# A two-layer MLP in seven-product form on one Trainium2 core: the second layer starts its products in another order

## The chip, the cores and the metric

The kernel runs on one core of a Trainium2 chip, in one launch. Its time is device microseconds (us) from start to end, the median of three runs. The core has TensorE (PE in the profile; PEld is its loading of weights), VectorE (DVE), ScalarE (ACT), GpSimd (POOL) and SyncE (SP), whose queue SPq issues the DMAs here. Each engine works through its own instructions in the order in which they were written down, and waits on semaphores for the others.

## The reference

An attention layer, a first MLP with a layer norm, and then the second MLP, of which this document tells:

```python
def _moe2_ref(x, w_in, w_out):          # x: 4608 x 512, w_in: 512 x 2048, w_out: 2048 x 512
    h = x @ w_in
    g = h * (1.0 / (1.0 + np.exp(-1.702 * h)))
    return (g @ w_out).astype(np.float32)
```

## The kernel before

The first part (attention and first MLP, until about 536 us) leaves x in HBM. The second part takes the 4608 tokens in 12 blocks of 384. Both matrix products of a block are done by a seven-product scheme: operands are cut into quarters (`Q11, Q21, Q22, Q12`), seven sums of quarters (called p1 to p7 here, by the number in the code) are multiplied instead of eight pairs. Each of the seven operands is held as two fp16 halves (a rounded value, "high", and what rounding left, "low"), and three matmuls (`PASSES`) make one product of them. A weight's seven forms are prepared once (`w2i`, `w2o`); the token side is made anew in each block.

**A block.** Its w_in product is cut into four units u0 to u3 (`Up`), each 256 hidden columns wide, and its w_out product is one unit dn (`Down`), which contracts over all four. A product of an Up unit is 12 matmuls (2 output halves x 2 slices x 3 passes), one of dn is 48 (8 slices k0 to k7; k0 and k1 need u0, k2 and k3 u1, and so on). So a block has 4 x 7 x 12 + 7 x 48 = 672 matmuls of 192 columns, all written at L1290, and one small fp32 matmul at L378.

**Accumulation.** PSUM bank a of a unit collects p1, then p6, p7 and p4 on top of it; bank b holds p2, bank d p5 and then p3. Between two products on bank a, ACT copies the sum so far into a quarter of the SBUF tile `c` (`snap`, L1300), and DVE adds bank b or d to a quarter (`add`, L1303). The next product on that bank has to wait for that copy. Q11 = p1+p2, Q12 = p1+p6+p5+p3, Q22 = p1+p6+p7+p5, Q21 = p1+p6+p7+p4.

**After an Up unit.** When `c` is whole, ACT computes the gated activation of all four quarters (`gate`, L1325) into slots 0 to 3 of a work tile `w_g`; slots 0 to 2 (`FIRST`) are the operands of p1, p2 and p3 as they stand, "direct quarters". Four subtractions on POOL (`combos`, L333 to L336; on DVE for u3) make slots 3 to 6 (`REST`), the operands of p7, p5, p6 and p4. ACT casts to fp16 high halves (`high`, L1334), DVE makes the low halves (`low`, L1337), each for FIRST and REST apart. dn multiplies them.

**The next block's tokens** (`nxt`) go through the same between the units: four DMAs load y (L355), DVE takes its largest value (L329) and makes a diagonal (L372), a matmul spreads it (L378, "spread"), DVE derives scales (L383 to L388, "rescale"), four subtractions on POOL make `w_y`, and ACT (L411) and DVE (L414) make the halves `ys`. The output of dn leaves by four DMAs on SP (`store`, L1364).

**Order.** The second part is in manual order: each engine's instructions stand as the code calls them in the loop below. Tiles rotate in pools: `psa` 3 banks, `psb` 2, `psd` 3, 3 buffers of `c`, 2 of `work`, 1 of each `g`; a tile's first writer waits for the last reader of the tile that held its buffer. In a block, PE's order is: u0 p1, p2; dn of the block before p7; u0 p6, p5; dn p4; u0 p7; dn p3; then for u1, u2, u3: p1, p2, (last unit's p4), p6, (last unit's p3), p5, p7; then dn p1 on k0 to k2 (18 matmuls), u3 p4, u3 p3, the rest of dn p1 and p2 on k0 to k3, p5 on k0 to k3, p1 and p2 on k4 to k7, p5 on k4 to k7, p6.

Of the kernel before, what the change touches and what calls it, by code (L numbers as in the profile page):

```python
# [8 lines left out]
F32 = mybir.dt.float32  # L9
# [9 lines left out]
P = 128  # L19
# [72 lines left out]
NS = 7  # L92
# [188 lines left out]
def moe_kernel(ctx: ExitStack, tc: tile.TileContext, qT, kT, vT, w_in, w_out, g_ln, w2_in, w2_out, eye, outT):  # L281
# [952 lines left out]
    with ExitStack() as ph:  # L1234
# [14 lines left out]
        class Unit:  # L1249


            def open(self, which, ks):
                k0 = ks[0] == 0
                for p in which:
                    if k0:
                        if p == 1:
                            self.a = psa.tile([P, 2, TH], F32, name="bank_a")
                            self.c = sb.tile([P, 4, 2, TH], F32, name="c")
                        elif p == 2:
                            self.b = psb.tile([P, 2, TH], F32, name="bank_b")  # L1260
                        else:
                            self.d = psd.tile([P, 2, TH], F32, name="bank_d")
                    last = ks[-1] == self.kc - 1
                    self.product(p, {1: "a", 2: "b", 5: "d"}[p], ks, k0, last)
                    if last and p == 1:
                        self.snap(Q11, self.a)
                    elif last and p == 2:
                        self.add(Q11, self.b)

            def more(self, p, begun=False):  # L1270
                self.product(p, "d" if p == 3 else "a", range(self.kc), False, True, True)
                if p == 6:
                    self.snap(Q12, self.a)
                elif p == 7:
                    if begun:
                        self.add(Q22, self.a)
                    else:
                        self.snap(Q22, self.a)
                        self.add(Q22, self.d)
                elif p == 4:  # L1280
                    self.snap(Q21, self.a)
                else:
                    self.add(Q12, self.d)

# [195 lines left out]
```

## Time and profile before

| | us |
|---|---|
| three timed runs | 1253.4, 1254.3, 1257.36 |
| median | 1254.3 |
| span of the profiled execution, first to last instruction | 1251.5 |
| first part, until the last matmul of its kind | about 536 |
| blocks 1 to 10, from u0's first product to the next block's | 58.8 each, three of them 59.0 to 60.8 |
| last block, to the last matmul | 69.9 |

For the profiled execution only its span is known, no time of its own around it; the span stands 2.8 us under the median of the runs. A row of a timeline gives start, duration, engine, line, operation, what it writes and reads, how many were merged, and in brackets how long the engine had been idle and who released it. A merged row of matmuls ends with the modelled end of the last; the rate is read from the starts of two rows that follow each other. The profiled clock is that of TensorE, 1.00 being 2.4 GHz.

### The profile page before, as it was taken

The page shows a single profiled execution, that of the slowest core. Times are in us where ns is not written, and L with a number is a line of the kernel's source. Part 1 is how long each engine was busy: PE and PEld are TensorE (multiplying, and loading weights), DVE is VectorE, ACT ScalarE, POOL GpSimd, SP SyncE. Part 2 cuts the span into 40 slices and gives each one's busy share as a digit, 9 for nine tenths or more (in the row PEclk, how much of TensorE's full clock was granted, in tenths as well). Part 3 has the DMA queues.
Part 4 walks back from the last instruction along what each step waited for, and adds up shares of the span by engine and source line. Part 5 has one row for each costly group of instructions (what it writes and reads, how often), then busy time and mean ns, then how long its engine had stood idle before and what let it go on. Part 6 is the DMA issues. An engine that isn't in the chain of part 4 may idle for free.

```text
span 1251.5 us, 27586 instructions
## 1 busy us (share of the span) xinstructions
PE 1143.5 (91%) x11678; PEld 989.6 (79%) x11678; DVE 730.9 (58%) x1153; ACT 766.5 (61%) x1073; POOL 664.7 (53%) x696
## 2 busy tenths in 40 slices
PE   2778998899999999889999999999999999999998
PEld 2335665576666666789999999999999898999998
DVE  7898877587677843136455454637272737364543
ACT  6998998788789855345445353627263536454552
POOL 5887998687879953424333352525262515243331
PEclk9989999899999999999999999999999999999999
DMA  9979999999989698470101010100011010101000
GB/s 324 302 205 240 269 270 256 248 231 248 256 206 234 164 230 236 109 270 8 46 14 39 14 40 20 33 27 27 27 33 46 7 46 8 46 7 46 14 14 26
DMA packets 246524, 152.85 MB, mean 122 GB/s; under 512 B 163584, under 2 KB 226176, under 8 KB 244096
## 3 DMA queue, kind: packets, MB, share of 16 engines
q1 hardware_dynamic: 246400, 151.09, 45.5%
q8 instruction: 91, 1.49, 0.5%
q14 instruction: 33, 0.27, 0.1%
HBM read 77.66 MB, written 33.55 MB: 89 GB/s over the span
## 4 chain that ended last, share of the span: by engine, by line
PE 30%; POOL 12%; DVE 8%; ACT 8%; issue 5%; DMA 0%; ACTq 0%; POOLq 0%
PE bank_a L1290 18%; PE bank_d L1290 8%; ACT w_g L1325 6%; DVE g L1337 5%; POOL w_g L336 3%; PE bank_b L1290 3%; POOL w_g L335 3%; POOL w_g L333 2%; POOL w_g L334 2%; PE psy L512 2%; ACT g L1334 1%; DVE c L1303 1%; POOL zs L475 1%; DVE w_g L333 0%; ACT c L1300 0%
## 5 line engine op out<-in xcount | busy, mean ns | idle before, releaser
L1290 PEld LDWEIGHTS <-w2i 128*128 128x128 f16 x4032 | 337.4, 98 | 34.3 <-issue 33.7
L1290 PEld LDWEIGHTS <-w2o 128*128 128x128 f16 x4032 | 335.0, 98 | 7.4 <-issue 6.8
L333 POOL TENSOR_TENSOR w_g<-w_g 128x384 f32<-128x384 f32 x36 | 43.6, 1211 | 379.3 <-ACT w_g L1325 379.3
L1290 PE MATMUL bank_a<-ys,w2i 128*128 128x192 f16 x2304 | 215.1, 247 | 27.1 <-ACT c L1300 25.0
L512 PE MATMUL psh<-w1i,xT 128*128 128x512 f16 x864 | 205.8, 389 | 8.9 <-DVE mean L475 8.2
L1290 PE MATMUL bank_a<-g,w2o 128*128 128x192 f16 x2304 | 206.0, 246 | 1.0
L512 PE MATMUL psy<-zT,w1o 128*128 128x256 f16 x1728 | 196.8, 273 | 8.8 <-ACT y L475 8.8
L512 PEld LDWEIGHTS <-w1o 128*128 128x128 f16 x1728 | 167.9, 98 | 35.8 <-issue 10.3
L1337 DVE SCALAR_TENSOR_TENSOR g<-w_g,gu_b,g 128x1152 f16<-128x1152 f32 (+1 forms) x96 | 169.1, 1782 | 24.5 <-ACT g L1334 24.4
L512 PEld LDWEIGHTS <-xT 128*128 128x128 f16 x864 | 84.4, 100 | 103.9 <-issue 13.8
L1300 ACT ACTIVATE c<-bank_a 128x384 f32<-128x384 f32 x192 | 91.7, 484 | 116.4 <-PE bank_a L1290 113.1
L1334 ACT ACTIVATE g<-w_g,gu_b 128x1152 f16<-128x1152 f32 (+1 forms) x96 | 132.9, 1408 | 39.4 <-POOL w_g L336 39.0
L1303 DVE SCALAR_TENSOR_TENSOR c<-bank_d,c 128x384 f32<-128x384 f32 x96 | 53.3, 555 | 134.4 <-ACT c L1300 99.5
L475 POOL TENSOR_TENSOR zs<-tt,zs 128x1024 f16<-128x1024 f32 x36 | 77.4, 2149 | 59.7 <-ACT zs L475 59.5
L1290 PE MATMUL bank_d<-ys,w2i 128*128 128x192 f16 x1152 | 107.5, 249 | 0.3 <-DVE c L1303 0.3
L1290 PE MATMUL bank_d<-g,w2o 128*128 128x192 f16 x1152 | 102.4, 246 | 3.0 <-DVE g L1337 3.0
L1325 ACT ACTIVATE w_g<-c,ch_b 128x1536 f32<-128x1536 f32 x48 | 75.3, 1568 | 36.8 <-DVE c L1303 36.7
L1300 ACT ACTIVATE c<-bank_a,co_b 128x384 f32<-128x384 f32 x47 | 26.9, 573 | 108.6 <-PE bank_a L1290 108.6
L512 PE MATMUL psx<-kbd,qt 128*128 128x144 f32 (+1 forms) x320 | 46.3, 306 | 24.6 <-ACT raw_z L475 12.7
L512 PEld LDWEIGHTS psx<-kbd,qt 128*128 128x128 f32 (+1 forms) x320 | 41.4, 193 | 29.4 <-issue 12.7
L475 POOL TENSOR_TENSOR lo<-w_f,hi 128x512 f16<-128x512 f32 (+1 forms) x46 | 62.2, 1365 | 2.7 <-ACT hi L475 2.3
L475 DVE TENSOR_REDUCE hmx<-psh 128x1 f32<-128x1024 f32 x36 | 43.7, 1214 | 34.1 <-PE psh L512 34.1
(189 smaller groups left out, 1693.1 us busy)
## 6 DMA issues: line engine op xcount, KB each, us to landing
raw<-w_out SPq DMA_DIRECT2D x12, 1024.0 KB, 6.9
raw<-w_in SPq DMA_DIRECT2D x10, 1024.0 KB, 8.0
half<-kT SPq DMA_DIRECT2D x16, 576.0 KB, 5.4
half<-vT SPq DMA_DIRECT2D x16, 576.0 KB, 5.5
qt<-qT SPq DMA_DIRECT2D x36, 256.0 KB, 3.9
y_dram<-y SPq DMA_DIRECT2D x36, 256.0 KB, 2.8
y<-y_dram SPq DMA_DIRECT2D x48, 192.0 KB, 3.2
outT<-c SPq DMA_DIRECT2D x48, 192.0 KB, 1.9
```

The costliest lines, as they stand in the source:

```text
L333: eng.tensor_tensor(out=w[:, 1], in0=q[:, Q12], in1=q[:, Q11], op=ALU.subtract)
L334: eng.tensor_tensor(out=w[:, 2], in0=q[:, Q22], in1=w[:, 1], op=ALU.subtract)
L335: eng.tensor_tensor(out=w[:, 0], in0=q[:, Q22], in1=q[:, Q12], op=ALU.subtract)
L336: eng.tensor_tensor(out=w[:, 3], in0=q[:, Q21], in1=w[:, 2], op=ALU.subtract)
L475: getattr(eng, name)(*args, **kw)
L512: nc.tensor.matmul(*p[:3], start=p[3], stop=p[4])
L1290: nc.tensor.matmul(bank[:, q], self.weight(p, q, kk, w), self.data(p, kk, i), start=(first and q == 0 and kk == 0 and w == 0 and i == 0), ...
L1300: nc.scalar.activation(out=self.c[:, i], in_=bank, func=AF.Copy, scale=self.scale)
L1303: nc.vector.scalar_tensor_tensor(out=self.c[:, i], in0=bank, scalar=self.scale, in1=self.c[:, i], op0=ALU.mult, op1=ALU.add)
L1325: nc.scalar.activation(out=self.w[:, 0:4], in_=self.c, func=AF.Gelu_apprx_sigmoid, scale=self.ch)
L1334: nc.scalar.activation(out=self.g[:, 0, s], in_=self.w[:, s], func=AF.Copy, scale=self.gu)
L1337: nc.vector.scalar_tensor_tensor(out=self.g[:, 1, s], in0=self.w[:, s], scalar=self.gu, in1=self.g[:, 0, s], op0=ALU.mult, op1=ALU.subtract,)
```

## The change

Only the order and a few operands in the second part change; the number of matmuls, of casts and of DMAs stays.

- **Up units**: u0 now runs p1, p2, p6, p5 in one go, then dn (of the block before) p7, then u0 p7. dn p4 stands later, after u0 p3 and u0's gate, ahead of u1 p5. dn p3 is no longer in the next block.
- **dn begins with p1, p2 and p3** on FIRST: p1 and p2 on k0 to k3 (48 matmuls) stand ahead of u3 p4; p3 on k0 to k3, p5 on k0 to k3, then p1, p2, p3 on k4, k5 and on k6, k7; then p6 and p5, which need REST. p5 has a bank of its own (e, from `psd`), and Q12 is put together by a copy of bank d and two adds, so there is one DVE add more in a block.
- **Casts**: the tile `g` of a unit is split into one for FIRST and one for REST. On ACT, u0's and u3's FIRST cast follows the gate at once; u2's REST cast stands ahead of u3's gate; u3's REST cast stands ahead of dn's copy of Q11.
- **nxt**: the four subtractions of the next block's tokens move from POOL to DVE, behind u3's REST low half. Its load is issued after dn's store on SP, its largest value is taken after u1's last add.

On ACT, this is the end of one block in the kernel before (the names `g_10986`, `g_11111` and `g_11193` are u1, u2 and u3; 1152 wide is FIRST, 1536 REST; `c<-bank_a,co_b` is a copy for dn, without `co_b` for an Up unit):

```order
L1334 ACTIVATE g_10986<-w_g,gu_b 128x1536
L1325 ACTIVATE w_g<-c,ch_b 128x1536
L1300 ACTIVATE c<-bank_a 128x384
L1334 ACTIVATE g_11111<-w_g,gu_b 128x1152
L1300 ACTIVATE c<-bank_a 128x384
L1325 ACTIVATE w_g<-c,ch_b 128x1536
L1334 ACTIVATE g_11193<-w_g,gu_b 128x1152
L1334 ACTIVATE g_11111<-w_g,gu_b 128x1536
L1334 ACTIVATE g_11193<-w_g,gu_b 128x1536
L411 ACTIVATE ys<-y,y_up 128x1152
L1300 ACTIVATE c<-bank_a,co_b 128x384
```

And the same place on ACT in the changed kernel (`g_3_11108` is u1's REST, `g_0_11157` and `g_3_11254` are u2's FIRST and REST, `g_0_11258` and `g_3_11354` u3's):

```order
L1345 ACTIVATE g_3_11108<-w_g,gu_b 128x1536
L1335 ACTIVATE w_g<-c,ch_b 128x1536
L1276 ACTIVATE c<-bank_a 128x384
L1345 ACTIVATE g_0_11157<-w_g,gu_b 128x1152
L1276 ACTIVATE c<-bank_a 128x384
L1345 ACTIVATE g_3_11254<-w_g,gu_b 128x1536
L1335 ACTIVATE w_g<-c,ch_b 128x1536
L1345 ACTIVATE g_0_11258<-w_g,gu_b 128x1152
L411 ACTIVATE ys<-y,y_up 128x1152
L1345 ACTIVATE g_3_11354<-w_g,gu_b 128x1536
L1276 ACTIVATE c<-bank_a,co_b 128x384
L1276 ACTIVATE c<-bank_d,co_b 128x384
```

u2's REST cast went from behind u3's FIRST cast to ahead of u3's gate, and the next tokens' first cast (`ys`) from behind u3's REST cast to ahead of it; dn's first copy (`co_b`) stays behind u3's REST cast.

On DVE, this is the end of a block before, from u3's last add on (`g_9485` is u2, `g_9567` u3; the four `w_g` rows are u3's combos):

```order
L1303 SCALAR_TENSOR_TENSOR c<-bank_d,c 128x384
L333 TENSOR_TENSOR w_g<-w_g 128x384
L334 TENSOR_TENSOR w_g<-w_g 128x384
L335 TENSOR_TENSOR w_g<-w_g 128x384
L336 TENSOR_TENSOR w_g<-w_g 128x384
L1337 SCALAR_TENSOR_TENSOR g_9567<-w_g,gu_b,g_9567 128x1152
L1337 SCALAR_TENSOR_TENSOR g_9485<-w_g,gu_b,g_9485 128x1536
L1337 SCALAR_TENSOR_TENSOR g_9567<-w_g,gu_b,g_9567 128x1536
L1303 SCALAR_TENSOR_TENSOR c<-bank_b,co_b,c 128x384
L414 SCALAR_TENSOR_TENSOR ys<-y,y_up,ys 128x1152
L414 SCALAR_TENSOR_TENSOR ys<-w_y,y_up,ys 128x1536
```

And in the changed kernel, from u2's REST low half on (`g_3_9616` is u2's REST, `g_0_9620` and `g_3_9716` are u3's FIRST and REST):

```order
L1350 SCALAR_TENSOR_TENSOR g_3_9616<-w_g,gu_b,g_3_9616 128x1536
L1350 SCALAR_TENSOR_TENSOR g_0_9620<-w_g,gu_b,g_0_9620 128x1152
L333 TENSOR_TENSOR w_g<-w_g 128x384
L334 TENSOR_TENSOR w_g<-w_g 128x384
L335 TENSOR_TENSOR w_g<-w_g 128x384
L336 TENSOR_TENSOR w_g<-w_g 128x384
L1350 SCALAR_TENSOR_TENSOR g_3_9716<-w_g,gu_b,g_3_9716 128x1536
L333 TENSOR_TENSOR w_y<-y 128x384
L334 TENSOR_TENSOR w_y<-y,w_y 128x384
L335 TENSOR_TENSOR w_y<-y 128x384
L336 TENSOR_TENSOR w_y<-y,w_y 128x384
L414 SCALAR_TENSOR_TENSOR ys<-y,y_up,ys 128x1152
```

u3's FIRST low half went ahead of u3's combos, u2's REST low half ahead of both, and the four subtractions for the next tokens (`w_y`), which POOL did before, stand between u3's REST low half and the tokens' first low half.

On PE, these are the last matmul of dn before u3 p4 and u3 p4's first in the kernel before (`w2o_6653` is p1's weight, `g_7734` belongs to u1, k2; `w2i_5791` is p4's):

```order
L1290 LDWEIGHTS w2o_6653
L1290 MATMUL bank_a<-g_7734,w2o_6653 128x192
L1290 LDWEIGHTS w2i_5791
L1290 MATMUL bank_a<-ys,w2i_5791 128x192
```

and in the changed kernel (`w2o_6654` is p2's weight, `g_0_8591` is u1's FIRST, k3):

```order
L1257 LDWEIGHTS w2o_6654
L1257 MATMUL bank_b<-g_0_8591,w2o_6654 128x192
L1257 LDWEIGHTS w2i_5791
L1257 MATMUL bank_a<-ys,w2i_5791 128x192
```

Ahead of u3 p4 there are now 48 matmuls of dn (p1 and p2 on k0 to k3) where 18 stood.

The diff, cut to the order of the loop and dn's new parts:

```diff
+            def early(self, which, ks):
+                for p in which:
...
+                    self.begin(p, bank, pool, ks)
+                    if ks[-1] == self.kc - 1:
+                        if p == 1:
+                            self.snap(Q11, "a")
+                        elif p == 2:
+                            self.add(Q11, "b")
+                        else:
+                            self.snap(Q12, "d")
+
+            def p6(self, ks):
+                self.more(6, "a", ks)
+                if ks[-1] == self.kc - 1:
+                    self.add(Q12, "a")
+
+            def p5(self, ks):
+                self.begin(5, "e", psd, ks)
+                if ks[-1] == self.kc - 1:
+                    self.add(Q12, "e")
...
-            u0.open((1, 2), ALL)
+            u0.p12()
+            u0.p6()
+            u0.p5()
             if dn:
-                dn.more(7)
-            u0.more(6)
-            u0.open((5,), ALL)
+                dn.p7()
+            u0.p7()
+            u0.out7()
+
+            u1.p12()
+            u0.p4()
+            u0.out4()
+            u1.p6()
+            u0.p3()
+            u0.out3()
+            u0.gate()
+            u0.high(FIRST)
+            u0.combos()
             if dn:
-                dn.more(4)
-            u0.more(7)
-            if dn:
-                dn.more(3)
+                dn.p4()
                 dn.store()
...
-            dn.open((1,), range(3))
+            dn.early((1, 2), range(4))
+            u3.p4()
+            u3.out4()
+            u3.p3()
+            u3.out3()
             u2.low(FIRST)
-            u3.more(4)
-            u3.more(3)
+            u2.high(REST)
             u3.gate()
             u3.high(FIRST)
-            u2.high(REST)
+            u2.low(REST)
+            u3.low(FIRST)
             u3.combos(nc.vector)
-            u3.low(FIRST)
-            u2.low(REST)
             if nxt:
-                nxt.combos(nc.gpsimd, work)
-            dn.open((1,), range(3, 4))
-            dn.open((2,), range(4))
+                nxt.high(FIRST)
+            dn.early((3,), range(4))
+            dn.p5(range(4))
+            dn.early((1, 2, 3), range(4, 6))
             u3.high(REST)
             u3.low(REST)
             if nxt:
-                nxt.high(FIRST)
...
+                nxt.combos(nc.vector, work)
+                nxt.low(FIRST)
+            dn.early((1, 2, 3), range(6, 8))
+            dn.p6(range(6))
+            dn.p5(range(4, 6))
             if nxt:
-                nxt.low(FIRST)
                 nxt.high(REST)
                 nxt.low(REST)
...
+            dn.p6(range(6, 8))
+            dn.p5(range(6, 8))
             tok = nxt
...
+        dn.p7()
+        dn.p4()
         dn.store()
```

## Rows read from the trace of the kernel before

**Rows 1.** Page, part 1: busy time, share of the span and instructions of each engine.
```profile
PE 1143.5 (91%) x11678; PEld 989.6 (79%) x11678; DVE 730.9 (58%) x1153; ACT 766.5 (61%) x1073; POOL 664.7 (53%) x696
```

**Rows 2.** Timeline of PE: where block 1 and block 11 begin, and the last product.
```profile
586.58 1.15 PE L1290 MATMUL bank_a<-ys,w2i 128*128 128x192 f16 x12
...
1178.07 1.15 PE L1290 MATMUL bank_a<-ys,w2i 128*128 128x192 f16 x12
...
1243.99 4.12 PE L1290 MATMUL bank_a<-g,w2o 128*128 128x192 f16 x48
```

**Rows 3.** Waits of PE in blocks 1 to 10: us in total, times, longest.
```profile
PE bank_a L1290 <- ACT c L1300: 17.6, 10, 2.2
```

**Rows 4.** Timeline of PE: two rows of a steady rate, the spread, the wait.
```profile
881.81 1.15 PE L1290 MATMUL bank_a<-ys,w2i 128*128 128x192 f16 x12
882.80 1.15 PE L1290 MATMUL bank_b<-ys,w2i 128*128 128x192 f16 x12
...
915.76 0.41 PE L378 MATMUL bank_b<-diag_y,ones 128*128 128x128 f32 x2
916.29 1.15 PE L1290 MATMUL bank_a<-ys,w2i 128*128 128x192 f16 x12
...
920.25 1.65 PE L1290 MATMUL bank_a<-g,w2o 128*128 128x192 f16 x18
923.53 1.15 PE L1290 MATMUL bank_a<-ys,w2i 128*128 128x192 f16 x12 [1.63 <-ACT c L1300]
```

**Rows 5.** Timeline, ACT and POOL ahead of that wait, one DVE cast among them.
```profile
912.79 1.56 ACT L1325 ACTIVATE w_g<-c,ch_b 128x1536 f32<-128x1536 f32 x1
914.43 1.49 POOL L333 TENSOR_TENSOR w_g<-w_g 128x384 f32<-128x384 f32 x1 [3.15 <-ACT w_g L1325]
916.00 1.00 POOL L334 TENSOR_TENSOR w_g<-w_g 128x384 f32<-128x384 f32 x1
916.75 1.46 DVE L1337 SCALAR_TENSOR_TENSOR g<-w_g,gu_b,g 128x1152 f16<-128x1152 f32 x1
916.95 2.12 POOL L335 TENSOR_TENSOR w_g<-w_g 128x384 f32<-128x384 f32 x1
...
920.06 1.58 ACT L1334 ACTIVATE g<-w_g,gu_b 128x1536 f16<-128x1536 f32 x1 [2.09 <-POOL w_g L336]
921.55 1.56 ACT L1325 ACTIVATE w_g<-c,ch_b 128x1536 f32<-128x1536 f32 x1
923.01 0.47 ACT L1300 ACTIVATE c<-bank_a 128x384 f32<-128x384 f32 x1
923.38 1.24 ACT L1334 ACTIVATE g<-w_g,gu_b 128x1152 f16<-128x1152 f32 x1
```

**Rows 6.** Lines by form, one block (881.8 to 940.6): DVE, mean ns of one.
```profile
L1337 DVE SCALAR_TENSOR_TENSOR g<-w_g,gu_b,g 128x1536 f16<-128x1536 f32 x4 | 7.2, 1814 | 1.3 <-ACT g L1334 1.3
L1303 DVE SCALAR_TENSOR_TENSOR c<-bank_d,c 128x384 f32<-128x384 f32 x8 | 4.4, 556 | 11.3 <-ACT c L1300 8.3 <-PE bank_d L1290 3.0
L333 DVE TENSOR_TENSOR w_g<-w_g 128x384 f32<-128x384 f32 x1 | 0.6, 559 | 1.7 <-ACT w_g L1325 1.7
```

**Rows 7.** Timeline: from a product's end (947.61) to its copy; SP's store and load.
```profile
947.61 1.15 PE L1290 MATMUL bank_d<-ys,w2i 128*128 128x192 f16 x12
947.81 0.49 ACT L1300 ACTIVATE c<-bank_a 128x384 f32<-128x384 f32 x1 [0.41 <-PE bank_a L1290]
...
964.95 1.90 SPq L355 DMA_DIRECT2D y<-y_dram  x4
...
971.74 1.75 DVE L329 TENSOR_REDUCE yam<-y 128x1 f32<-128x1536 f32 x1 [1.59 <-DMA y<-y_dram]
```

**Rows 8.** Tile outT, 930 to 1060 us: from issue to landing of nine stores.
```profile
DMA to landing us min/median/max: 1.9/1.9/3.0
```

**Rows 9.** Timeline of PE: dn's first product in block 0.
```profile
566.55 1.65 PE L1290 MATMUL bank_a<-g,w2o 128*128 128x192 f16 x18
```

**Rows 10.** Window behind a 2.01 us wait: each engine's busy time, clock, DMA, GB/s.
```profile
806.00:808.00 2.00, 2.00 (x17) 1.92 (x16) 1.78 (x1) 0.68 (x2) 2.00 (x2) 0.57 0.00 0
```

More of the change, by code (lines that the diff above doesn't have):

```diff
@@ L1249, in moe_kernel @@
         class Unit:
[L1252 to L1283, printed above, removed]
             def product(self, p, bank, ks, first, last, again=False):
@@ L1327, in gate @@
                 )
-                self.g = gp.tile([P, 2, NS, 2, TH], F16, name=f"g{self.u}")
+                self.g = {}
             def combos(self, eng=nc.gpsimd):
@@ L1357, in data, with p7, p4 @@
             def data(self, p, kk, i):
-                return self.ups[kk // 2].g[:, i, B_OF[p], kk % 2, :]
+                s = B_OF[p]
+                of = FIRST if s < FIRST.stop else REST
+                return self.ups[kk // 2].g[of.start][:, i, s - of.start, kk % 2, :]
+            def early(self, which, ks):
+                for p in which:
+                    if p == 1 and ks[0] == 0:
+                        self.c = sb.tile([P, 4, 2, TH], F32, name="c")
+                    bank, pool = {1: ("a", psa), 2: ("b", psb), 3: ("d", psd)}[p]
+                    self.begin(p, bank, pool, ks)
+                    if ks[-1] == self.kc - 1:
+                        if p == 1:
+                            self.snap(Q11, "a")
+                        elif p == 2:
+                            self.add(Q11, "b")
+                        else:
[8 more added lines that the diff above has]
+                    self.add(Q12, "e")
+            def p7(self):
+                self.more(7, "a")
+                self.snap(Q22, "a")
+                self.add(Q22, "e")
+            def p4(self):
+                self.more(4, "a")
+                self.snap(Q21, "a")
             def store(self):
@@ L1375, in moe_kernel @@
+            u0.out7()
[8 more added lines that the diff above has]
+            u0.combos()
             if dn:
-                dn.more(4)
-            u0.more(7)
-            if dn:
-                dn.more(3)
+                dn.p4()
                 dn.store()
-            p1, p2 = u0, None
+            u0.low(FIRST)
+            u1.p5()
+            u1.p7()
@@ L1382, in moe_kernel @@
+            u1.out7()
             if b:
[L1383 to L1408 removed]
@@ L1409, in moe_kernel @@
-            dn = Down(b, ups, tok)
-            dn.open((1,), range(3))
+                nxt = Tokens(b + 1, sb, "c") if more_to_come else None
+            u2.p12()
+            u0.high(REST)
+            u0.low(REST)
+            u1.p4()
+            u1.out4()
+            u2.p6()
+            u1.p3()
+            u1.out3()
+            u1.gate()
+            u1.combos()
+            if nxt:
+                nxt.largest(sb.tile([P, P], F32, name="diag_y", bufs=1))
+            u2.p5()
+            u2.p7()
@@ new lines, in moe_kernel @@
+            u2.out7()
+            u1.high(FIRST)
+            u3.p12()
+            u1.low(FIRST)
+            u2.p4()
+            u2.out4()
+            if nxt:
+                nxt.spread(psb.tile([P, 2, TH], F32, name="bank_b"))
+            u3.p6()
+            u1.high(REST)
+            u2.p3()
+            u2.out3()
+            u2.gate()
+            u1.low(REST)
+            u2.combos()
+            u3.p5()
+            u3.p7()
+            u3.out7()
+            u2.high(FIRST)
+            if nxt:
+                nxt.rescale()
```

84 lines of the change are left out of this document (39 added, 45 removed).

## The prediction

> **What bounds the kernel now.** I read the shares of the engines first: PE is busy 91% of the span, no other engine over 61%, though PEld, the weight loading beside the matmuls, reaches 79% [rows 1]. So a change of order can only give back time in which PE stands. The change touches the second part alone, so next I cut that part into its blocks: block 1 begins at 586.58 us, block 11 at 1178.07, the last product at 1243.99 [rows 2]. Ten blocks take 591.5, 59.15 each. Two products of 12 matmuls that follow each other start 0.99 us apart, 82.5 ns per matmul, and the spread takes 0.53 (915.76 to 916.29) [rows 4]. A block's 672 matmuls need 55.44, with the spread 55.97. So PE loses 3.2 us in a block, and that is all there is to win there: 32 us in ten blocks.
>
> Who holds PE? In these ten blocks it waits 17.6 us in ten waits, about one a block, for ACT's copies out of bank a [rows 3]. The timeline names the place: dn's first 18 matmuls start at 920.25 and would be through at 921.7, but u3's p4 starts only at 923.53, since the copy of u3's Q22, which frees bank a, runs at 923.01 [rows 4, 5]. That copy is short. It is late because ACT works in order: ahead of it stand u1's REST cast (920.06), which waited 2.09 us for POOL, and u2's gate (921.55) [rows 5]. POOL is late because its four subtractions, 1.00 us each undisturbed, took from 914.43 to 920.03: the third lasted 2.12 beside a DVE cast, the first 1.49. Once, behind such a wait of 2.01 us, the granted clock was 0.57 over the next two us [rows 10], the lower level of 1.2 GHz for most of them; blocks with that are longer than 58.8.
>
> **The change part by part.** Times with a plus count from the block's first matmul in the new order, as if PE never stood: 0.99 per Up product, 3.96 per product of dn, 0.53 for the spread.
>
> *The wait removed.* Up to u2's p3 stand 24 Up products, p7 and p4 of the dn before and the spread: it ends at +32.2. A copy or add starts 0.20 behind the product (947.61 to 947.81) [rows 7]; the add takes 0.56 [rows 6]; so u2's gate could start at +33.1. ACT is still busy: u1's p3 ends at +24.75, its gate runs +25.6 to +27.2, POOL's four subtractions then take 4.1 undisturbed, 5.6 in the disturbed rows; I take 5.2 (one of them at 2.12, since u1's FIRST low half runs in that time). That is +32.4, u1's REST cast (1.58 [rows 5]) ends at +34.0, u2's gate at +35.5, the copy of u3's Q22 at +36.0. u3's p4 stands behind 48 matmuls of dn where there were 18 and so comes at +38.2: the wait goes, with 2.2 us to spare. The other small ones (u2's p4 behind ACT and dn's p5 behind a DVE cast) go the same way: between the copy and the product on its bank there is now always another product. Only u0's p1, p2, p6 stand close: 0.20 + 0.49 + about 0.05 against p2's 0.99, hidden.
>
> *What is late next.* u2's FIRST cast (1.24) ends at +37.2. POOL starts u2's subtractions at +35.6 and needs 4.1 to 5.6; only the tail of u1's REST low half (to about +35.9) runs beside it, so I take 4.5, as with the row of 1.49: +40.1. Now u2's REST cast stands ahead of u3's gate, and the gate, ready at +40.9 (u3's p3 ends at +40.1), starts at +41.7 and ends at +43.2; u3's FIRST cast ends at +44.4. DVE has u2's FIRST low half (1.46) from +40.9 and its REST low half (1.81 [rows 6]) to +44.2, so u3's FIRST low half ends at +45.9; dn's p1 on k6 needs it at +47.1: hidden. u3's subtractions on DVE (four of 0.56 that overlap a little: 2.1) end at +48.0, u3's REST cast at +49.6, and only then comes dn's copy of Q11 (0.56 for a copy by co_b, I take the add's length): +50.1. dn's p6, on the same bank, stands at +50.0. So the two meet. With POOL at 4.1 the cover is 0.3 us; at 5.6 the wait is 1.2. I take 0.3 a block, nearer the undisturbed row, for that and for small gaps.
>
> *The subtractions moved from POOL to DVE.* Four of 0.56 against rows of 1.00 to 2.12. u3's REST low half ends at +51.4, the four at +53.5, the tokens' FIRST low half at about +55.1 (1.63 at most, between FIRST's 1.46 and REST's 1.81), REST's at +57.5 behind the cast and an add. The next block's p1 comes at +56.3, its p6 at +58.3. Nothing waits, with about 1 us of cover; beyond it, each us late costs one a block. The one add more (0.56) lies in DVE time that is idle.
>
> *The store and the load behind it.* dn's p4 now ends at +17.8 of the next block, its copy at +18.6, and SP then issues the fourth store and four loads of y in order. The stores land in 1.9 to 3.0 [rows 8], at +20.6 to +21.7; the copy of u2's Q11 takes over that buffer of c and is due at +21.0; u2's p6 needs it started by +22.2: hidden. The loads are issued from +19.0; before, the largest value could start 6.8 us after the first issue (964.95 to 971.74) [rows 7], so here at +25.8. It takes 1.75, the diagonal less than an add's 0.56, and the spread comes at +29.7: 1.6 us of cover.
>
> *Sum.* Blocks 1 to 10: 55.97 + 0.3 = 56.27 instead of 59.15, minus 28.8. Block 0: its order on PE is the same up to dn's first product (566.55 [rows 9]), though u0's FIRST cast (1.24) now stands ahead of a copy on ACT that u1's p4 awaits; that costs between nothing and 1.2, I take 0.5. Behind it stand 264 matmuls, p3 among them: 21.8 + 0.3, so block 1 begins at 589.1, plus 2.5. Last block: from 1178.07 to the end of the last product at 1243.99 + 3.96 are 69.9; now 768 matmuls, 63.4, and p4 directly behind p7 on bank a, which waits for the copy between them (0.20 + 0.56 + 0.05 = 0.8), and 0.3: 64.5, minus 5.4. Together minus 31.7: the span goes from 1251.5 to 1219.8. The median of the runs stands 2.8 above the span; with the same distance, 1222.6, so 1223.
>
> **The rivals.** (1) *The late chain shows.* u2's subtractions on POOL are disturbed as u1's are, 1.1 us more, and all that follows in order on ACT (u2's cast, u3's gate and casts, the copy of Q11) shifts by it: dn's p6 waits 1.2 to 1.4 in each of twelve blocks, 13 us more than the forecast, 1236. For it: the cover is nothing. Against it: beside POOL then run only adds and scales of DVE, and in the rows a subtraction slowed only beside a cast. The Trainium skill's page "SBUF — State Buffer", section "Who interferes with whom", says that a DVE instruction with two inputs in SBUF and a GpSimd instruction that reads SBUF hold each other up whole, and that one with at most one SBUF input does not; the low half has two, an add from PSUM one. By that rule rival 1 needs u1's REST low half to come late by a us; the subtraction of 2.12 beside a low half agrees with it.
>
> (2) *The wait only moves.* If both POOL's sets are slow (1.5 each) and ACT's casts queue up behind them, dn's p6 waits 3 us a block and nothing is won: 1254, no change.
>
> (3) *Slower: the store holds u2.* The copy of u2's Q11 waits for four stores, now issued only at +18.6. It has until +22.2, 3.6 after the issue, against 1.9 to 3.0 measured. Each us beyond stops PE at u2's p6 in eleven blocks; from a landing of 6.5 us on the gain is eaten (2.9 a block), at 8 the time is 1223 + 48 = 1271. Against it: the DMA engines do hardly anything else then.
>
> **How the numbers follow.** Forecast 0.62 (its own range 1217 to 1230: the wait at dn's p6 from nothing to 0.8 a block, block 0 by its bounds); rival 1 0.24 (1230 to 1245); rival 2 0.06; rival 3 0.06; 0.02 for something better. The range 1214 to 1241 holds the forecast and most of rival 1. Two of this kernel's runs differ by up to 0.3% (3.8 us), so less than that is no change: faster 0.88, same 0.05, slower 0.07.
>
> **What would show it.** Right: u0's first products 56 to 56.5 us apart, no wait of PE at u3's p4, the granted clock 1.00 throughout the second part, POOL idle at a block's end, dn's p6 starting within 0.5 us of the end of p3. Wrong: a wait of PE on bank a or d of over 1 us in each block (dn's p6 for rival 1 and 2, u2's p6 behind DMA for rival 3, the spread behind the load), or DVE's low halves for the next tokens ending after their matmuls are due.

## The result and the profile after

The changed kernel takes 1221.71 us (median of 4 runs, 1219.39 to 1224.68), the kernel before 1255.83 beside it: a ratio of 0.9731, 95% interval 0.9711 to 0.9751. The forecast was 1223 with a range of 1214 to 1241. The profiled run took 1221.39 us, with a span of 1219.6. Lines have moved: a product's matmuls are L1257 now, the copies L1276, the adds L1279, the gate L1335, the casts of an Up unit L1345 (ACT) and L1350 (DVE).

The page's first part (busy time, share of the span, instructions) answers to [rows 1]: DVE has 40 us more and POOL 88 less, and PE's share has risen from 91% to 93%.

```profile
PE 1137.7 (93%) x11678; PEld 989.5 (81%) x11678; DVE 771.2 (63%) x1209; ACT 774.7 (64%) x1073; POOL 576.4 (47%) x652
```

PE's timeline at the places of [rows 2] (block 1, block 11, the last product) and, under it, PE's waits from 539 us to the end (us in total, times, longest) and one window over blocks 1 to 10 (length, busy time of PE, PEld, DVE, ACT and POOL, granted clock, DMA share, GB/s):

```profile
594.70 1.15 PE L1257 MATMUL bank_a<-ys,w2i 128*128 128x192 f16 x12
...
1151.69 1.15 PE L1257 MATMUL bank_a<-ys,w2i 128*128 128x192 f16 x12
...
1212.05 4.12 PE L1257 MATMUL bank_a<-g,w2o 128*128 128x192 f16 x48 [0.67 <-ACT c L1276]
```
```profile
PE bank_a L1257 <- ACT c L1276: 8.1, 6, 3.4
```
```profile
594.70:1151.69 556.99, 556.99 (x6742) 556.79 (x6741) 341.07 (x451) 295.03 (x340) 142.35 (x120) 1.00 0.10 30
```

Ten blocks take 556.99 us, 55.70 each instead of 59.15, and in them PE has no idle time and a granted clock of 1.00; the list of its waits between 600 and 1150 us is empty, where [rows 3] had ten. All six waits that are left stand at the part's two ends. So the span's 31.9 us come from three places: 34.5 from blocks 1 to 10 (591.5 to 557.0), 5.5 from what follows them (73.4 to 67.9), and 8.1 are given back ahead of block 1, which begins at 594.70 instead of 586.58. Of these, 3.1 lie ahead of u0's p6 of block 0, the first product behind the first part's last: it began at 539.07 before and at 542.14 here, in both behind a wait of 3.42 us. The change does not touch the first part, and in seven experiments below that begin alike this product began anywhere between 536.42 and 541.15; the trace here is the latest of all, so it is likely, but not shown, that these 3.1 are chance. The other 5.0 are block 0 itself (from that product to block 1, 47.51 before, 52.56 here).

The timeline of one block's end (PE, ACT, POOL and DVE; the block began at 928.93), behind two rows of the spread in the block before, is where the prediction's chain can be checked.

```profile
902.95 0.41 PE L378 MATMUL bank_b<-diag_y,ones 128*128 128x128 f32 x2
903.20 1.15 PE L1257 MATMUL bank_a<-ys,w2i 128*128 128x192 f16 x12
...
964.37 0.47 ACT L1276 ACTIVATE c<-bank_a 128x384 f32<-128x384 f32 x1
964.54 1.17 POOL L333 TENSOR_TENSOR w_g<-w_g 128x384 f32<-128x384 f32 x1 [3.15 <-ACT w_g L1335]
...
966.80 1.15 PE L1257 MATMUL bank_a<-ys,w2i 128*128 128x192 f16 x12
967.70 1.00 POOL L336 TENSOR_TENSOR w_g<-w_g 128x384 f32<-128x384 f32 x1
968.73 1.58 ACT L1345 ACTIVATE g<-w_g,gu_b 128x1536 f16<-128x1536 f32 x1 [0.25 <-POOL w_g L336]
...
976.55 1.57 ACT L1345 ACTIVATE g<-w_g,gu_b 128x1536 f16<-128x1536 f32 x1 [2.34 <-DVE w_g L336]
978.03 0.56 ACT L1276 ACTIVATE c<-bank_a,co_b 128x384 f32<-128x384 f32 x1
978.68 3.13 PE L1257 MATMUL bank_a<-g,w2o 128*128 128x192 f16 x36
...
979.89 0.55 DVE L333 TENSOR_TENSOR w_y<-y 128x384 f32<-128x384 f32 x1
...
983.75 1.81 DVE L414 SCALAR_TENSOR_TENSOR ys<-w_y,y_up,ys 128x1536 f16<-128x1536 f32 x1
```

The old block that [rows 4] shows took 58.80 us, 3.1 more than a new one. Of these, 1.8 are the wait at u3's p4 and 0.28 lie behind the spread, both in [rows 4]; 0.22 stand ahead of u2's p4 at 914.77, 0.26 inside dn's p1 on k6 and k7, and 0.50 inside dn's p5, which waits for a low half of u3 on DVE (13 matmuls, 1.07 us of work, take 1.57 here):

```profile
934.18 1.24 PE L1290 MATMUL bank_d<-g,w2o 128*128 128x192 f16 x13
935.75 1.07 PE L1290 MATMUL bank_d<-g,w2o 128*128 128x192 f16 x11 [0.33 <-DVE g L1337]
```

So the wait at u3's p4 is somewhat more than half of what the change gave back in such a block.

In the changed kernel the copy of u3's Q22 ends at 964.84 and u3's p4 comes at 966.80: the old wait is gone, with 2.0 us to spare. At dn's p6 there is next to nothing to spare: the copy of Q11 on its bank ends at 978.59, the product starts at 978.68.

### The profile page after: what moved, and what is told of

It reads as the page before. It is cut to its first block, busy times and chain, and to the rows that moved or that the text cites. A ratio compares the mean times of both kernels' runs of the same rounds, so it can differ in the third digit from the quotient of the medians.

```text
span 1219.6 us, 27576 instructions
## 1 busy us (share of the span) xinstructions
PE 1137.7 (93%) x11678; PEld 989.5 (81%) x11678; DVE 771.2 (63%) x1209; ACT 774.7 (64%) x1073; POOL 576.4 (47%) x652
## 4 chain that ended last, share of the span: by engine, by line
PE 64%; POOL 15%; DMA 6%; DVE 6%; ACT 5%; issue 3%; SPq 1%; DVEq 0%; ACTq 0%; POOLq 0%
PE bank_a L1257 30%; PE bank_d L1257 15%; PE bank_b L1257 7%; PE psy L512 6%; PE psh L512 5%; POOL w_f L475 4%; POOL lo L475 3%; POOL zs L475 2%; DMA half<-kT 2%; POOL st L475 2%; DMA half<-vT 1%; POOL q L475 1%; POOL e L475 1%; ACT he L475 1%; DVE hmx L475 1%
## 5 line engine op out<-in xcount | busy, mean ns | idle before, releaser
L1257 PEld LDWEIGHTS <-w2i 128*128 128x128 f16 x4032 | 335.3, 98 | 8.2 <-issue 7.9
L1257 PEld LDWEIGHTS <-w2o 128*128 128x128 f16 x4032 | 333.4, 98 | 1.8 <-issue 1.6
L333 POOL TENSOR_TENSOR w_g<-w_g 128x384 f32<-128x384 f32 x36 | 39.1, 1087 | 496.2 <-ACT w_g L1335 496.2
L1350 DVE SCALAR_TENSOR_TENSOR g<-w_g,gu_b,g 128x1152 f16<-128x1152 f32 x96 | 168.9, 1768 | 90.5 <-ACT g L1345 90.5
L1257 PE MATMUL bank_a<-ys,w2i 128*128 128x192 f16 x2304 | 212.5, 247 | 6.9 <-ACT c L1276 6.8
L512 PE MATMUL psy<-zT,w1o 128*128 128x256 f16 x1728 | 200.4, 276 | 8.8 <-ACT y L475 8.8
L1257 PE MATMUL bank_a<-g,w2o 128*128 128x192 f16 x2304 | 203.8, 246 | 1.3 <-ACT c L1276 1.3
L1276 ACT ACTIVATE c<-bank_a 128x384 f32<-128x384 f32 x192 | 93.1, 487 | 149.2 <-PE bank_a L1257 145.6
L1345 ACT ACTIVATE g<-w_g,gu_b 128x1152 f16<-128x1152 f32 x96 | 135.6, 1413 | 48.8 <-DVE w_g L336 29.2
L1257 PE MATMUL bank_d<-ys,w2i 128*128 128x192 f16 x1152 | 107.4, 247 | 0.0
L1257 PE MATMUL bank_d<-g,w2o 128*128 128x192 f16 x1152 | 104.8, 246 | 0.0
L1279 DVE SCALAR_TENSOR_TENSOR c<-bank_d,c 128x384 f32<-128x384 f32 x96 | 53.5, 557 | 69.6 <-PE bank_d L1257 48.6
L1335 ACT ACTIVATE w_g<-c,ch_b 128x1536 f32<-128x1536 f32 x48 | 75.3, 1568 | 27.1 <-DVE c L1279 27.1
L1279 DVE SCALAR_TENSOR_TENSOR c<-bank_b,c 128x384 f32<-128x384 f32 x48 | 26.7, 557 | 61.4 <-ACT c L1276 38.6
L475 POOL TENSOR_TENSOR lo<-w_f,hi 128x512 f16<-128x512 f32 (+1 forms) x46 | 62.5, 1369 | 3.2 <-ACT hi L475 2.0
```

What stands on the lines that cost most here:

```text
L333: eng.tensor_tensor(out=w[:, 1], in0=q[:, Q12], in1=q[:, Q11], op=ALU.subtract)
L475: getattr(eng, name)(*args, **kw)
L512: nc.tensor.matmul(*p[:3], start=p[3], stop=p[4])
L1257: nc.tensor.matmul(bank[:, q], self.weight(p, q, kk, w), self.data(p, kk, i), start=(first and q == 0 and kk == 0 and w == 0 and i == 0), ...
L1276: nc.scalar.activation(out=self.c[:, i], in_=getattr(self, bank), func=AF.Copy, scale=self.scale)
L1279: nc.vector.scalar_tensor_tensor(out=self.c[:, i], in0=getattr(self, bank), scalar=self.scale, in1=self.c[:, i], op0=ALU.mult, op1=ALU.add,)
```

## The experiments

In each, the short diff is against the changed kernel, if nothing else is said; "block" is the distance of u0's first products in the steady blocks, 55.69 us in the changed kernel.

**The moved subtractions.** First, they go back to POOL and all else stays.

```diff
-                nxt.combos(nc.vector, work)
+                nxt.combos(nc.gpsimd, work)
```

> The changed kernel with the next tokens' four subtractions on POOL again, at the same place in the order. My theory: POOL can start them as soon as u2's work tile is free, beside u3's own subtractions on DVE, and the two engines hold each other up, so the late chain (u3's subtractions, REST cast, copy of Q11, dn's p6), which has no cover left (0.05 us), gets 1 to 2 us longer and PE waits that long at dn's p6 in ten or eleven blocks: 1232 to 1242. Rival, that moving them off POOL is nothing, since POOL is idle there: blocks of 55.69, 1222.

Measured: 1251.68 us (1250.21 to 1258.72), ratio to before 0.9999 (0.9981 to 1.0017); blocks of 58.3, two of ten 60.0. The whole gain is gone. The timeline of one block's end, DVE, POOL, ACT and PE:

```profile
936.66 1.99 POOL L334 TENSOR_TENSOR w_y<-y,w_y 128x384 f32<-128x384 f32 x1
937.72 1.35 DVE L333 TENSOR_TENSOR w_g<-w_g 128x384 f32<-128x384 f32 x1
938.61 1.31 POOL L335 TENSOR_TENSOR w_y<-y 128x384 f32<-128x384 f32 x1
939.10 1.24 DVE L334 TENSOR_TENSOR w_g<-w_g 128x384 f32<-128x384 f32 x1
...
942.11 1.57 ACT L1345 ACTIVATE g<-w_g,gu_b 128x1536 f16<-128x1536 f32 x1 [5.00 <-DVE w_g L336]
943.59 0.56 ACT L1276 ACTIVATE c<-bank_a,co_b 128x384 f32<-128x384 f32 x1
944.20 3.13 PE L1257 MATMUL bank_a<-g,w2o 128*128 128x192 f16 x36 [2.46 <-ACT c L1276]
```

POOL's subtractions for the tokens run beside u3's on DVE, and both are slow: 1.24 to 1.35 us where DVE needs 0.56 alone (its fourth, when POOL is through, takes 0.54), 1.31 to 1.99 where POOL needs 1.00. u3's REST cast waits for DVE, the copy of Q11 stands behind that cast, and dn's p6 waits 2.46 us for the copy. So what rival 2 of the prediction forecast, a wait that only moves to dn's p6 and nothing won, is what the new order does without this one line. It comes about in another way than rival 2 had it: POOL's subtractions for u2 take 1.17, 1.00, 0.99 and 1.00 in this block, as in the changed kernel, and the slow set is u3's on DVE.

Second, the same line alone, in the kernel before (ratios are to the kernel before):

```diff
-                nxt.combos(nc.gpsimd, work)
+                nxt.combos(nc.vector, work)
```

> The kernel before with one part of the change alone: the four subtractions of the next tokens run on DVE instead of POOL, the order stays. Theory: the old order loses its time at u3's p4, behind u1's subtractions on POOL, with which the tokens' have nothing to do; so the move alone gains little, and the order and the move are worth their 33 us only together: 1248 to 1256, blocks of 58.3 to 58.9. Rival: the move itself is the gain, as putting it back cost all of it: 1224 to 1240, blocks under 58.

Measured: 1283.41 us (1280.09 to 1289.46), ratio 1.023 (1.0198 to 1.0262), blocks of 60.9, some of 62.5. The old wait stays, as expected; that nothing else is lost was wrong. The timeline, DVE and PE at a block's end:

```profile
942.08 1.15 PE L1290 MATMUL bank_a<-ys,w2i 128*128 128x192 f16 x12 [1.70 <-ACT c L1300]
...
954.54 1.81 DVE L1337 SCALAR_TENSOR_TENSOR g<-w_g,gu_b,g 128x1536 f16<-128x1536 f32 x1
...
956.41 1.07 PE L1290 MATMUL bank_d<-g,w2o 128*128 128x192 f16 x11 [2.45 <-DVE g L1337]
```

In this kernel the tokens' subtractions stand on DVE ahead of u3's REST low half, and dn's p5 on that half comes so early that it waits 2.45 us for it, besides the 1.70 at u3's p4. The four kernels make a table: old order, POOL 1; old order, DVE 1.023; new order, POOL 0.9999; new order, DVE 0.9731. As run, neither half of the change gains anything alone; together they gain 2.7%. The loss in the old order comes from the place, though: in the changed kernel the subtractions stand behind u3's REST low half, and the old order with them there was not run. That it would gain nothing either is likely, since none of the waits of the old block, listed above, is for the tokens, but it is not shown.

Third, the subtractions on POOL, but held there until u3's REST cast is done.

```diff
-                nxt.combos(nc.vector, work)
+                behind = sb.tile([P, 4], F16, name="behind", bufs=1)
+                nc.gpsimd.tensor_copy(out=behind, in_=u3.g[REST.start][:, 0, 0, 0, 0:4])
+                nxt.combos(nc.gpsimd, work)
```

> The changed kernel with the next tokens' four subtractions on POOL again, but held there until u3's REST cast is done (by a tiny copy of four columns on POOL that reads what that cast wrote), so that they can no longer run beside u3's four subtractions on DVE. Theory: it is the overlap of the two sets that cost all the gain when POOL had them unheld, so most of it is kept: dn's p6 does not wait for the copy of Q11; what is left is that POOL's four now run beside u3's REST low half and the tokens' FIRST low half, end about +54 to +55.5 into the block, and hold the tokens' REST cast and u0's p6 by nothing to 1.2 us a block: 1222 to 1236. Rival: POOL is too slow for these subtractions wherever they stand: 1245 to 1254.

Measured: 1237.45 us (1233.43 to 1239.8), ratio 0.987 (0.9839 to 0.99), blocks of 57.34. The timeline of POOL and DVE at a block's end, and under it PE's waits from 600 to 1150 us:

```profile
983.65 1.82 DVE L1350 SCALAR_TENSOR_TENSOR g<-w_g,gu_b,g 128x1536 f16<-128x1536 f32 x1 [1.64 <-ACT g L1345]
983.83 2.51 POOL L333 TENSOR_TENSOR w_y<-y 128x384 f32<-128x384 f32 x1
985.40 2.15 DVE L414 SCALAR_TENSOR_TENSOR ys<-y,y_up,ys 128x1152 f16<-128x1152 f32 x1
986.41 2.00 POOL L334 TENSOR_TENSOR w_y<-y,w_y 128x384 f32<-128x384 f32 x1
```
```profile
PE bank_a L1257 <- DVE ys L414: 11.1, 9, 1.2
```

dn's p6 no longer waits, as expected, and half of the gain is back. POOL's first two subtractions now run beside the two low halves, take 2.51 and 2.00, and u0's p6, which needs the tokens' REST low half, waits 1.2 us for it. The median lies 1.5 above the range I gave (POOL's four ended at 990.31, +57.5 into the block that began at 932.78, not at +55.5). So it matters when POOL does this work, but POOL's four are long and met a low half or a subtraction on DVE at both places that were tried; on DVE they are through in 2.1 us.

**The cover at u3's p4.** Only 18 matmuls of dn stand ahead of u3's p4, as before the change; the other 30 follow u3's p3.

```diff
-            dn.early((1, 2), range(4))
+            dn.early((1,), range(3))
...
             u3.out3()
+            dn.early((1,), range(3, 4))
+            dn.early((2,), range(4))
```

> The changed kernel with one thing undone: ahead of u3's p4 stand again 18 matmuls of dn (p1 on k0 to k2) and not 48; the other 30 follow u3's p3. My theory, that both the longer cover and the earlier copy on ACT removed the wait: in the changed kernel the copy of u3's Q22 ends 2.0 us after dn's first matmul, 18 matmuls last 1.49, so u3's p4 waits about 0.55 us in each block, blocks of 56.25 instead of 55.69, time 1222 + 12 x 0.55 = 1229. Rival, that the cover alone did it and ACT is as late as before: the old wait of 1.6 us returns, blocks of 57.3, time about 1241. Rival, that neither mattered: 1222.

Measured: 1226.86 us (1224.23 to 1229.11), ratio 0.9786 (0.9758 to 0.9814), blocks of 56.25. In the steady blocks PE waits at u3's p4 alone, in each as in this one:

```profile
742.96 1.15 PE L1257 MATMUL bank_a<-ys,w2i 128*128 128x192 f16 x12 [0.40 <-ACT c L1276]
```

With the copy as early as it is now, the 30 matmuls of cover are worth 0.56 us a block; the rest of the old wait (1.8 a block in the mean) is gone already because the copy comes earlier, 2.0 us behind dn's first matmul (962.84 to 964.84) where it was 3.2 (920.25 to 923.48). The two overlap: 48 matmuls last 3.96, so by these rows the longer cover could have hidden the old copy by itself. A kernel with that cover and the old order on ACT was not run.

**The cover at dn's p6.** One subtraction more on POOL, ahead of u2's four (it repeats one that has been done).

```diff
             u1.low(REST)
+            nc.gpsimd.tensor_tensor(out=u2.w[:, 4], in0=u2.w[:, Q12], in1=u2.w[:, Q11], op=ALU.subtract)
             u2.combos()
```

> The changed kernel with one subtraction more on POOL (about 1.0 us, done twice to the same result) ahead of u2's four: a dose on the late chain. My theory: the copy of dn's Q11 ends 0.05 us before dn's p6 needs it, so nearly the whole us shows there, 0.9 a block, blocks of 56.6, time about 1222 + 12 x 0.9 = 1233. Rival, that the chain has slack elsewhere (u3's gate waits for u3's last add and not for u2's cast): 0 to 0.5 a block, under 1228.

Measured: 1234.22 us (1229.9 to 1235.26), ratio 0.9841 (0.9816 to 0.9867), blocks of 56.73. A microsecond of POOL there costs 1.03 us a block, and PE pays it at dn's p6:

```profile
986.38 3.13 PE L1257 MATMUL bank_a<-g,w2o 128*128 128x192 f16 x36 [0.88 <-ACT c L1276]
```

So the chain u2's subtractions, u2's REST cast, u3's gate and casts, u3's subtractions, u3's REST cast, copy of Q11 has no slack; had rival 1's 1.1 us more on POOL come about, its price of 13 us would have been about right. The same dose, with the last 12 matmuls of p1 and the copy of Q11 written ahead of u3's REST cast:

```diff
             dn.early((1, 2, 3), range(4, 6))
+            dn.early((1,), range(6, 8))
             u3.high(REST)
             u3.low(REST)
+            dn.early((2, 3), range(6, 8))
...
-            dn.early((1, 2, 3), range(6, 8))
```

> The same with one subtraction more, and dn's copy of Q11 ahead of u3's REST cast on ACT (the last part of dn's p1 is written before that cast, p2 and p3 behind it). My theory, that the dose costs only because the copy stands behind the cast: dn's p6 no longer waits, blocks of 55.7 to 55.9 (the next tokens' halves come within 0.2 us of their matmuls), 1222 to 1225. Rival, that the dose acts by another way (the low halves of u3 themselves too late for dn's p1 or p6): as without this, 1233.

Measured: 1226.93 us (1224.23 to 1228.61), ratio 0.9788 (0.9765 to 0.981), blocks of 56.10. The wait at dn's p6 is gone, and 0.41 a block is left, at u0's first products, which wait for the tokens' low halves on DVE: the FIRST half ends at 934.56, and u0's p1, begun at 934.28, takes 1.24 us to the next row instead of 0.99; the REST half ends at 936.70, and p6, begun at 936.51, takes 1.14.

```profile
934.28 1.40 PE L1257 MATMUL bank_a<-ys,w2i 128*128 128x192 f16 x12
935.52 1.15 PE L1257 MATMUL bank_b<-ys,w2i 128*128 128x192 f16 x12
```
```profile
933.15 1.41 DVE L414 SCALAR_TENSOR_TENSOR ys<-y,y_up,ys 128x1152 f16<-128x1152 f32 x1
934.88 1.82 DVE L414 SCALAR_TENSOR_TENSOR ys<-w_y,y_up,ys 128x1536 f16<-128x1536 f32 x1 [0.31 <-ACT ys L411]
```

That is the copy's place in ACT's queue, shown: at least 0.62 of the dose's 1.03 were paid only because it stood behind a cast. The edit also puts DVE's add of p2 to Q11 (0.61 us) ahead of the tokens' subtractions, so a part of the 0.41 is its own.

**The split of g.** The two parts of g are one tile again, as before the change.

```diff
-                self.g = {}
+                self.g = gp.tile([P, 2, NS, 2, TH], F16, name=f"g{self.u}")
...
```

> The changed kernel with g of a unit in one tile again, so that u0's FIRST cast, the first writer of the next g, must wait for the last reader of the old one instead of the last reader of its FIRST part alone. Theory: the split carries a part of the gain, since that cast stands ahead of copies on ACT and now waits for the end of dn's p4; ACT comes about 1.5 us late there, and the fourth store and the loads behind it by the same. Between nothing and 1.0 us a block shows on PE: 1222 to 1233, and the cast is listed as waiting for PE in each block. Rival: the split buys nothing because the cast is needed late anyway: 1222, blocks of 55.7.

Measured: 1220.72 us (1217.9 to 1226.27), ratio 0.9731 (0.9697 to 0.9764), blocks of 55.69. My theory falls. ACT around u0's FIRST cast:

```profile
943.58 1.25 ACT L1344 ACTIVATE g<-w_g,gu_b 128x1152 f16<-128x1152 f32 x1 [0.31 <-PE bank_a L1257]
945.01 0.58 ACT L1276 ACTIVATE c<-bank_a,co_b 128x384 f32<-128x384 f32 x1 [0.17 <-PE bank_a L1257]
```

The cast waits only 0.31 us, and the copy behind it waits for its own product anyway. The split is worth nothing here.

**The ends.** Five of the six waits that the changed kernel still has, on PE's timeline, with the ACT rows behind two of them:

```profile
541.59 0.49 ACT L1276 ACTIVATE c<-bank_a 128x384 f32<-128x384 f32 x1 [2.20 <-DMA y_dram<-y]
542.14 2.06 PE L1257 MATMUL bank_a<-ys,w2i 128*128 128x192 f16 x12 [3.42 <-ACT c L1276]
...
552.57 1.28 ACT L1335 ACT_TABLE_LOAD   x1 [1.16 <-DVE c L1279]
...
557.15 2.14 PE L1257 MATMUL bank_a<-ys,w2i 128*128 128x192 f16 x24 [1.32 <-ACT c L1276]
...
563.03 2.14 PE L1257 MATMUL bank_a<-ys,w2i 128*128 128x192 f16 x24 [1.57 <-ACT c L1276]
...
566.64 1.15 PE L1257 MATMUL bank_a<-ys,w2i 128*128 128x192 f16 x12 [0.48 <-ACT c L1276]
...
588.76 3.13 PE L1257 MATMUL bank_a<-g,w2o 128*128 128x192 f16 x36 [0.64 <-ACT c L1276]
```

The sixth is the 0.67 before the last product. Three kernels try to mend them. In the first, a dummy instruction loads the Gelu table early, block 0's casts of u0 stand behind the copies, and p5's last 24 matmuls stand between p7 and p4 at the end.

```diff
+        early_table = sb.tile([P, 4], F32, name="early_table", bufs=1)
+        nc.scalar.activation(out=early_table, in_=tok.ch, func=AF.Gelu_apprx_sigmoid)
...
-            u0.high(FIRST)
+            if dn:
+                u0.high(FIRST)
...
             u1.out7()
+            if not dn:
+                u0.high(FIRST)
+                u0.low(FIRST)
...
-        dn.p7()
+        dn.more(7, "a")
+        dn.snap(Q22, "a")
+        dn.p5(range(6, 8))
+        dn.add(Q22, "e")
```

> The changed kernel with its two ends mended: the Gelu table is loaded by a dummy instruction before the first block, in block 0 the casts of u0 stand behind the copies of the same stretch, and in the last block 24 matmuls of p5 stand between p7 and p4. Theory: the stalls of 1.32, 1.57 and 0.48 us at block 0 were casts and the table load ahead of copies, and the 0.67 at the end was the copy between p7 and p4; all of these go, the 3.42 at the start of the part stays: 3.4 to 4.7 us less than the changed kernel, 1217 to 1218.5, block 0 about 3.4 shorter, blocks 1 to 10 unchanged at 55.7. Rival: the casts delayed in block 0 are needed as soon as they move, and the stall appears on the next product instead: 1221 to 1222.

Measured: 1219.52 us (1213.74 to 1221.23), ratio 0.971 (0.9683 to 0.9737). Block 0 lost 2.2 us (52.56 to 50.39, from u0's p6 to block 1), less than expected, since two other waits appear there (0.37 for a copy, 0.97 for the spread's data) and the granted clock stays low for longer: 0.50 from 542 to 548 us, where the changed kernel has 0.55 and 0.60 from 542 to 546 and 1.00 behind that. At the end p7 now waits for DVE's add at 1205.49, so nothing is won there. The timeline, ACT and PE:

```profile
540.54 1.28 ACT L1416 ACT_TABLE_LOAD   x1 [2.19 <-DMA y_dram<-y]
...
542.47 2.08 PE L1257 MATMUL bank_a<-ys,w2i 128*128 128x192 f16 x12 [4.80 <-ACT c L1276]
...
1205.49 4.12 PE L1257 MATMUL bank_a<-g,w2o 128*128 128x192 f16 x48 [0.78 <-DVE c L1279]
```

The dummy instruction took over the wait for the first part's store, and the table load came behind it instead of before: PE waits 4.80 instead of 3.42. In the second kernel, the pools are laid out in another order besides:

```diff
-        wp, sb, gp, work = pool("w2", 1), pool("sb2", 3), pool("gp", 1), pool("work", 2)
+        wp, gp, work, sb = pool("w2", 1), pool("gp", 1), pool("work", 2), pool("sb2", 3)
```

> As the one with mended ends, and the second part's pools laid out in another order, so that the first buffer of c no longer lies on memory from which a store of the first part is still being read. Theory: the 3.42 us that PE waits at the start of the second part come from the first copy waiting for that store; here it waits for nothing but its product, so 2.5 to 3.5 us more go: 1214 to 1215.5. Rival: some other wait for the first part's memory takes its place (the load of y or of w2): 1217 to 1219, the same as with mended ends alone.

Measured: 1217.02 us (1214.14 to 1219.31), ratio 0.9697 (0.9671 to 0.9724). The wait of 4.80 is gone, but the first part has a new one. SP's queue and PE:

```profile
522.65 1.58 SPq L355 DMA_DIRECT2D y<-y_dram  x3
...
524.84 3.64 SPq L504 DMA_TRANSPOSE zT<-zs  x1
...
532.05 7.08 PE L512 MATMUL psy<-zT,w1o 128*128 128x256 f16 x48 [3.00 <-DMA zT<-zs]
```

The loads of block 1's tokens, free of their buffer earlier, now stand ahead of a transpose that the first part waits for. The third kernel puts these loads inside block 0, takes the tokens' largest value ahead of u0's REST low half there, and spreads p5 over both sides of p7.

```diff
-        nxt = Tokens(1, sb, "c")
...
-            if b:
-                nxt = Tokens(b + 1, sb, "c") if more_to_come else None
+            nxt = Tokens(b + 1, sb, "c") if more_to_come else None
...
+        dn.p5(range(4, 6))
         dn.more(7, "a")
```

> As the one with mended ends and other pools, with what that one still showed at its ends mended too: block 1's tokens are loaded inside block 0 (so that these loads no longer stand in SP's queue ahead of the first part's last transposes), their largest value is taken ahead of u0's REST low half in block 0, and in the last block 12 matmuls of p5 stand on either side of p7. Theory: the 3.0 us that PE waited for a transpose in the first part were the price of the early loads; they go, and with them the 0.98 at the first spread and the 0.8 near the end: 3 to 4.8 us less than with other pools alone, 1212 to 1214.5. Rival: the wait at the transpose belongs to the first part and varies from kernel to kernel: 1215 to 1217.

Measured: 1220.44 us (1218.06 to 1222.52), ratio 0.9731 (0.9706 to 0.9755). The transpose no longer holds PE and the end runs without a wait, but all is lost again at the first spread: behind seven loads of weights in SP's queue, the tokens come late, so the 1212 to 1214.5 that I expected is missed. SP, DVE and PE:

```profile
542.04 4.11 SPq L504 DMA_DIRECT2D w2o<-w2o_dram  x7
546.57 7.69 SPq L355 DMA_DIRECT2D y<-y_dram  x4
...
566.03 1.75 DVE L329 TENSOR_REDUCE yam<-y 128x1 f32<-128x1536 f32 x1 [10.32 <-DMA y<-y_dram]
...
568.25 0.77 PE L378 MATMUL bank_b<-diag_y,ones 128*128 128x128 f32 x2 [7.94 <-DVE diag_y L372]
```

The version with other pools is the fastest measured; its interval reaches into that of the changed kernel, so its 4 us are likely, not settled. Loads that stand between the last transpose and the weights were not tried.

## Why the prediction was right

**What bounded the kernel.** Right: PE stood behind ACT's copy, and nothing but PE's standing was there to win. The estimate of it was low: the spread costs 0.25 us here (902.95 to 903.20). The 0.53 of [rows 4] is what it took in each of the old order's nine blocks from 620 to 1095 us, but 0.28 of that was not its own cost (likely PE standing for the ACT copies that begin at 915.77, next to it), so a block without waits takes 55.69, not 55.97. The term "55.97 + 0.3" is 55.70: minus 34.5 instead of minus 28.8 for ten blocks. Both the spread and the 0.3 for waits and gaps were too large.

**The wait removed.** Right, with its place and cover: 2.0 us to spare at u3's p4 against 2.2 worked out. The run with 18 matmuls of cover shows what the cover is worth; that, by the rows, either the earlier copy or the cover would have removed most of the wait alone is not in the prediction.

**What is late next.** Right: the chain was walked to a copy ending at +50.1 with dn's p6 at +50.0, and the two do meet. The copy ends 0.4 earlier, at +49.66, and p6 starts 0.25 earlier, at +49.75, so instead of a wait of 0.1 there is a cover of 0.1. The choice of 4.5 us for u2's subtractions was a little high (964.54 to 968.70 is 4.16): u1's REST low half does run beside POOL's first subtraction, until 964.85, but that one takes only 1.17. The Trainium skill's page "SBUF — State Buffer", section "Who interferes with whom", has it that a DVE instruction with two SBUF inputs, as the low half is, disturbs POOL, and that one with at most one, outside DVE's two-port modes, does not; the trace agrees: of POOL's subtractions for u1 in this block, the second (957.36) takes 1.00 with an add from PSUM beside it (958.05, 0.56), the fourth (959.28) 2.11 with a low half beside it (958.52, 2.01). The prediction left out the part on two-port modes and counted the scales among what is harmless; a scale of [128 x 4] (966.73) did not slow POOL, whose subtraction beside it took 1.00, but itself took 1.04 us. Whether it runs in such a mode no run shows.

**The subtractions moved to DVE.** This is the step that was read too lightly. "Nothing waits, with about 1 us of cover" was right, and DVE has them done from 979.89 to 981.97. But I asked only what the move costs on DVE, not what the subtractions would have cost had they stayed: on POOL, beside u3's subtractions, 2.6 us a block (58.3 against 55.7), and 60.0 in two blocks of ten in which the clock fell behind the wait: the whole gain. Without this line the forecast would have been wrong by all of its gain.

**Store and load.** Right: the four stores land in 2.0 us (median; 3.7 the longest, from 600 to 1150 us), and no product of u2 waits; rival 3 did not come about.

**Block 0.** The size was wrong: plus 2.5 was forecast, 8.1 came. Of that 3.1 lie ahead of the block, likely the first part's differences from run to run. Block 0 itself takes 5.0 more, twice the forecast: it has four waits of 1.32, 1.57, 0.48 and 0.64, of which I had allowed for 0.8 in all. I had seen that u0's FIRST cast stands ahead of a copy, but not that the Gelu table load of 1.28 stands there too, nor that the REST cast does the same two products later.

**The last block.** Right: 64.3 us from u0's first product to the last matmul's end, 64.5 forecast, and 0.67 for p4 behind p7 where 0.8 was worked out.

So the time came out 1.3 us from the forecast, and the span 0.2 (1219.8 forecast, 1219.6 measured), because two errors of 5 to 6 us, in the ten blocks and ahead of them, have opposite signs. The mechanism was right, the closeness of the sum was luck. Two of the signs named for "right" did not come either: the blocks are 55.7 us apart, not 56 to 56.5, and the granted clock was not 1.00 throughout, but 0.55 and 0.60 from 542 to 546 us.

## What to carry to other kernels

When an order is changed so that a wait gets cover, walk the chain on to the next point where two engines meet, and ask of every line moved along both questions: what it costs at its new place, and what it would cost at its old one under the new order; here each half of the change alone, as it was run, was worth nothing or a loss. A copy that frees a bank should not stand behind a cast on an engine that works in order. Waits at the start and the end of a part appear once, but they can be larger than a block's (3.42 us here against 1.6 to 2.2), and in all three attempts here, curing one handed a wait to another instruction.

## What the hardware showed

Two sets of subtractions, each with both inputs in SBUF, ran beside each other on DVE and POOL and slowed each other: from 0.56 us to between 1.24 and 1.35 on DVE, and from 1.00 to between 1.31 and 1.99 on POOL. They come close to taking turns: in the run that held POOL's subtractions back, the first of them (983.83 to 986.34) ends 0.87 us behind a low half on DVE (until 985.47) and takes 1.00 alone, and DVE's next low half ends 1.21 behind it, at 987.55, and takes 1.41 alone. Even a scale of [128 x 4] on DVE took 1.04 us beside a POOL subtraction in the changed kernel (ten of ten in blocks 1 to 10), and 0.22 in each block of the old order, where POOL had finished or was within 0.06 us of its end. In the second part the granted clock fell only behind waits, in the four traces read two us at a time (the kernels before and after, and the two with only the subtractions moved): in the changed kernel after the wait of 3.42 us, to 0.55 from 542 to 544 us (1.2 GHz for most of it); and in the old order with the subtractions on DVE, behind the wait of 2.45 us in some blocks and not in others, to 0.67 and then 0.50 from 648 to 652 us.
